# One decode step of cached attention beside an MLP: all pairs in the loops, K awaited by TensorE, K folded in two chunks

## The chip, the cores and the metric

The kernel runs on one core of one Trainium2 chip. A core has a matrix engine (TensorE, in the profile PE, its weight loads PEld), three engines for elementwise work (VectorE = DVE, ScalarE = ACT, GpSimd = POOL), a sync engine (SyncE = SP) that here only issues transfers, and 16 DMA engines that bring data from HBM into the on-chip memory. The engines run their own instruction streams and meet at semaphores. The metric is the device time of one execution in microseconds.

## The reference

One token for each of 8 sequences passes attention over a cache of 4096 keys in 32 heads of 128, and an MLP; both are added to the input. K and V together are 2 x 8 x 32 x 4096 x 128 bf16 numbers, 537 MB.

```python
x = A_x                                  # (8, 1, 640) bf16
xn = _layernorm(x)
q = (xn @ wq) -> (8, 32, 1, 128)
scores = einsum("bhqd,bhkd->bhqk", q, k_cache) * 128 ** -0.5
o = einsum("bhqk,bhkd->bhqd", softmax(scores), v_cache)
y = _layernorm(xn)
out = x + o.reshape(8, 1, 4096) @ wo + gelu(y @ w1 + b1) @ w2 + b2
```

## The kernel before

**Pairs.** The work is cut into 32 pairs i = (group of 8 heads, sequence). A pair has 8 heads x 4096 keys; its K is a tile of 128 partitions x 256 columns x 128 numbers, 8.4 MB, and so is its V. Each partition holds 256 keys of one head (16 partitions a head). K goes alternately to the slots KA and KB, V to the one slot VS.

**One pair.** GpSimd spreads the query (`qrep`), TensorE turns it into one row per partition (`pe_qbc`), ScalarE copies it out of PSUM (`act_qbc`). The scores of the last 80 of the 256 columns come from TensorE: ten tiles of eight columns are transposed (`pe_T`), evacuated by ScalarE (`act_T`) and multiplied by the query (`pe_QK`); VectorE masks and sums these products (`dve_sel`). The scores of the first 176 columns come from VectorE: in chunks, K times the query in place, a first addition of halves, and a reduction (`dve_chunk`, three chunks of 58, 59 and 59 columns). Then VectorE finds the maxima and writes one bias per head (`dve_max`), ScalarE takes eight exponentials with their sums (`act_exp`), TensorE adds the sums over partitions (`pe_RS`) and multiplies the probabilities with V in 256 small products (`pe_PV`), VectorE inverts the sum (`dve_rinv`), ScalarE copies the product (`act_O`) and GpSimd scales it (`o_norm`).

**Order.** Each step is entered in a list with a position, `at(position, step, ...)`, 100 for a pair; sorted by position, the list gives each engine's order. In the stretch of pair i, ScalarE has the exponentials of pair i-1 (position 90 of the pair before) ahead of the tiles of pair i, TensorE the tiles of pair i ahead of the PV product of pair i-1. Pair 0 is the exception: its exponentials stand at `o + Q + 45`, behind the tiles of pair 1.

**Transfers.** SP issues in the order K(i+1), V(i), K(i+2), V(i+1). K(i) waits until TensorE and VectorE have finished with pair i-2 (`kt`, `km`), V(i) until the PV product of pair i-1 has ended. K1 and V0 wait for the last product of Q with wq (`qw`). TensorE does not wait for K itself: GpSimd waits for the transfer, writes one word (`k_ready`, the tile `kr_sb`), and TensorE waits for that write.

**Loops.** The steps are first recorded as calls, then replayed. ScalarE and VectorE replay pairs 0 and 1 as straight code and the pairs from 2 on in a loop of 15 turns of two pairs (`LOOP0, LOOPN = 2, 15`, `_replay_loop`). TensorE replays pair 0's first part as straight code and then loops (`_replay_pe`): in turn r the first part of pair r (query, tiles), then the sums and PV of pair r-1, and in the last but one turn a block of the end's products, skipped in the others. Semaphore values that grow from turn to turn are computed from the turn's number.

**Head and end.** Before pair 0 come the two norms, the spread of w1 into the layout that TensorE wants (`spread_w1`, five instructions on VectorE and five on ScalarE), the MLP, and Q. At the end the outputs of the first 24 heads are regrouped by products (`pe_sel`) that VectorE folds (`dve_fold`), and multiplied with wo; the last eight follow after PV(31). All instructions are emitted by one helper, so the profile puts nearly all of them on line 111; tiles tell them apart.

Of the kernel before, what the change touches and what calls it, by code (L numbers as in the profile page):

```python
# [14 lines left out]
P = 128  # L15
# [12 lines left out]
class _Eng:  # L28
# [17 lines left out]
    def sig(self, inst):  # L46
        self.n += 1
        inst.call[3] = (self.sem, 1)
        return (self.sem, self.n)

    def wait(self, *tickets):
        best = {}
        for t in tickets:
            if t is None:
                continue
            if isinstance(t, list):
                for u in t:
                    if u is not None:
                        best[u[0]] = max(best.get(u[0], 0), u[1])
            else:  # L60
                best[t[0]] = max(best.get(t[0], 0), t[1])
        for sem, n in best.items():
            if n > self.waited.get(sem, 0):
                self.waited[sem] = n
                self.wait_ge(sem, n)

# [96 lines left out]
def _replay_pe(e, calls, head, mid, end, late):  # L163

    n = len(head)
    first = [calls[a:b] for a, b in zip(head, mid)]
    second = [calls[a:b] for a, b in zip(mid, head[1:] + [end])]
    g1, g2 = _steps(first[:-1]), _steps([[c for c in t if not _late(c, late)] for t in second])
    _replay(e, calls[:head[0]])
    with e.bass.Fori(1, n + 1, engines=OrderedEngineSet([e.engine])) as r:  # L170
        reg = e.to_reg(r)
        with e.If_lt(reg, n):
            for call, step in zip(first[0], g1):
                _emit(e, call, call[1][1] + (r - 1) * step if step else None, r)
        g = iter(g2)
        for call in second[0]:
            if _late(call, late):
                e.wait_ge(call[1][0], (r >> (n.bit_length() - 1)) * 16 + 1)
            else:
                step = next(g)  # L180
                _emit(e, call, call[1][1] + (r - 1) * step if step else None)
        with e.If_eq(reg, n - 1):
            _replay(e, first[-1])
# [8 lines left out]
def bass_parallel_sum__gqa_block_cached__mixer_channel_mlp__decode_kernel(  # L192
# [29 lines left out]
    LOOP0, LOOPN = 2, 15  # L222
# [19 lines left out]
    group0 = [0]  # L242
    for i_ in range(NQ):
        group0.append(group0[-1] + jp_of(i_) // TPB)
# [4 lines left out]
    with ExitStack() as es:  # L249
# [23 lines left out]
        w2_sb = scratch(F * D // P + 2 * PAD)  # L273
# [13 lines left out]
        iota_h = scratch(2 * HS).bitcast(I32)  # L287
        mtmp = scratch(2 * 2 * HS).bitcast(F32).rearrange("p (w n) -> p w n", w=2)
        ones_sb = scratch(B, 1)
        zeros_sb = scratch(P)  # L290
# [3 lines left out]
        Sd_sb = sb("Sd_sb", [P, 2, NKEY], F32)  # L294
# [3 lines left out]
        qbc_sb = sb("qbc_sb", [P, 2, DH], BF)  # L298
        oT_sb = sb("oT_sb", [P, H, B], BF)
        oS_sb = sb("oS_sb", [P, NL, HS, B], BF)  # L300
        oU_sb = sb("oU_sb", [P, 2, HS], F32)
# [3 lines left out]
        mx_sb = sb("mx_sb", [P, 32], F32)  # L305
        mxT_sb = sb("mxT_sb", [P, 32], F32)
        mq_sb = sb("mq_sb", [P, 2], F32)
        mb_sb = sb("mb_sb", [P, 32], F32)
        mbT_sb = sb("mbT_sb", [P, 32], F32)
        NB_sb = sb("NB_sb", [P, 2, HS], F32)  # L310
# [3 lines left out]
        kr_sb = sb("kr_sb", [P, 1], F32)  # L314
# [25 lines left out]
        tk = {}  # L340
# [12 lines left out]
        def load_k(i):  # L353
            s = kslot(i)
            if i >= 2:
                sp.wait(tk[("kt", i - 2)], tk[("km", i - 2)])
            elif s == KB:
                sp.wait(tk["qw"])
            tk[("k", i)] = ld_s[s].sig(sp.dma_start(tile[s], cache_src(A_k_cache, i)))

# [13 lines left out]
        def load_wl(q):  # L374
            sp.wait(tk[("kt", NQ - 2)], tk[("km", NQ - 2)])
# [12 lines left out]
        def consts_pool():  # L388
            pool.iota(iota_h, [[-HP, HS]], base=0, channel_multiplier=1)
            tk["iota"] = pool.sig(pool.iota(iota_i, [[1, P]], base=0, channel_multiplier=-1))  # L390
            for d, (ap, v) in zip([None] * (6 - len(ld_vl)) + ld_vl, (
                    (zeros_sb, 0.0), (w2_sb[:, 0:PAD], 0.0), (w2_sb[:, PAD + F * D // P:], 0.0), (ones_sb, 1.0),
                    (mx_sb[:, :], 0.0), (mb_sb[:, :], 0.0))):
# [5 lines left out]
        def sel_pool():  # L399
            pool.wait(tk["id"], tk[("kt", NQ - 2)], tk[("km", NQ - 2)])  # L400
# [23 lines left out]
        def idents():  # L424
            dve.wait(tk["iota"])
            tk["id"] = dve.sig(dve.tensor_scalar(ident_bf[:, :], iota_i, 0.0, None, ALU.is_equal))
            dve.tensor_scalar(mtmp[:, 0, :], iota_h, 0.0, None, ALU.is_ge)
            t = dve.sig(dve.tensor_scalar(mtmp[:, 1, :], iota_h, float(HP), None, ALU.is_lt))
            dve.wait(t)
            t = dve.sig(dve.tensor_tensor(mask_sb[:, :], mtmp[:, 0, :], mtmp[:, 1, :], ALU.mult))  # L430
            dve.wait(t)
            tk["mask"] = dve.sig(dve.tensor_scalar(off_sb[:, :], mask_sb[:, :], 1.0, 1e30, ALU.subtract, ALU.mult))
            dve.wait(tk["id"])
# [40 lines left out]
        def spread(eng, dst, src, w):  # L474
            n = src.shape[1]
            for k in range(n):
                s_ = src[:, k, :].rearrange("p (q r) -> p r q", r=FQ)[:, w * FH:w * FH + FH + 1, :]
                d_ = dst[:, k, :, :].rearrange("p j (q w) -> p w j q", w=2)[:, w, :, :]
                last = eng.activation(d_, s_, ACT.Copy) if eng is act else eng.tensor_copy(d_, s_)
            return eng.sig(last)  # L480

        def spread_w1(w):
            eng = act if w else dve
            eng.wait(tk["w1"])
            tk[("w1r", w)] = spread(eng, w1r_sb, w1_sb, w)

        def spread_b1():
            pool.wait(tk["b1"])
            for w in range(2):
                tk["b1r"] = spread(pool, b1r_sb, b1_sb, w)  # L490

        def pe_mlp1():
            pe.wait(tk[("w1r", 0)], tk[("w1r", 1)], tk["b1r"], tk["consts"], tk[("xT", 1)])
# [13 lines left out]
        def dve_h():  # L507
            dve.wait(tk["h"], tk["par"])
            for w in range(2):
                last = dve.tensor_scalar(hh_sb[:, w, :, :], hT_sb[:, :, :], par_sb[:, w:w + 1], None, ALU.mult)  # L510
            tk["hh"] = dve.sig(last)
# [13 lines left out]
        def qrep(i):  # L525
            hq, b = divmod(i, B)
            pool.wait(tk["q"], tk.get(("qb_pe", i - 1)), tk.get(("qkl", i - 1)))
            tk[("qrep", i)] = pool.sig(pool.tensor_copy(
                qrep_sb[:, :, :],
                qT_sb[:, hq * HS:(hq + 1) * HS, b][:, :, None].to_broadcast([P, HS, HP])))  # L530

        def k_ready(i):
            pool.wait(tk[("k", i)])
            tk[("kr", i)] = pool.sig(pool.memset(kr_sb[:, :], 0.0))

        def pe_qbc(i):
            pe.wait(tk[("qrep", i)], tk["id"])
# [5 lines left out]
        def act_qbc(i):  # L543
            act.wait(tk.get(("ym", i - 2)))
            QBB.use(act)
            tk[("qb", i)] = QBB.used(act, act.sig(act.activation(
                qbc_sb[:, i % 2, :], QB_ps[:, 0:DH], ACT.Copy)))

        def pe_T(i, t):
            n = group0[i] + t  # L550
            k = n % 2
            j0 = NKEY - jp_of(i) + t * TPB
            pe.wait(tk["id"], tk[("kr", i)])
# [6 lines left out]
        def act_T(i, t):  # L560
            n = group0[i] + t
            k = n % 2
            act.wait(tk.get(("qk", n - NS)))
# [8 lines left out]
        def pe_QK(i, t):  # L572
            n = group0[i] + t
# [12 lines left out]
        def dve_chunk(i, c):  # L586
# [6 lines left out]
                kt, kt, qbc_sb[:, s, :][:, None, :].to_broadcast([P, w, DH]), ALU.mult))  # L593
# [3 lines left out]
            dve.wait(t, tk.get(("exp", i - 2)))  # L597
            tk[("km", i)] = dve.sig(dve.tensor_reduce(Sd_sb[:, s, lo:hi], kt[:, :, 0:DH // 2], AX.X, ALU.add))

        def dve_sel(i, f):  # L600
# [4 lines left out]
            dve.wait(tk["mask"], tk.get(("exp", i - 2)))  # L605
# [6 lines left out]
                Sd_sb[:, s, j0:j0 + hw], sp_, AX.X, ALU.add)))  # L612

        def dve_max(i):
            s = i % 2
            dve.wait(tk[("s", i)], tk[("km", i)], tk["consts"])
            t = dve.sig(dve.tensor_reduce(mx_sb[:, 0:1], Sd_sb[:, s, :], AX.X, ALU.max))
# [10 lines left out]
            dve.wait(t, tk.get(("exp", i - 2)))  # L628
            tk[("nb", i)] = dve.sig(dve.tensor_scalar(
                NB_sb[:, s, :], off_sb[:, :], mbT_sb[:, 0:1], None, ALU.add))  # L630

        def act_exp(i):
            s = i % 2
            act.wait(tk[("nb", i)], tk.get(("pv", i - 1)))
            for h in range(HS):
                last = act.activation(P_sb[:, h, :], Sd_sb[:, s, :], ACT.Exp, bias=NB_sb[:, s, h:h + 1],
# [9 lines left out]
        def dve_rinv(i):  # L646
            if i < 0:
                tk[("ri", i)] = CHB.used(dve, dve.sig(dve.tensor_copy(ri_sb[:, i % 2, :], off_sb[:, :])))
                return
# [19 lines left out]
        def act_O(i):  # L669
            if i < 0:  # L670
                act.wait(tk["mask"])
                tk[("oU", i)] = PVB.used(act, act.sig(act.activation(oU_sb[:, i % 2, :], off_sb[:, :], ACT.Exp)))
                return
            PVB.use(act)
            tk[("oU", i)] = PVB.used(act, act.sig(act.activation(oU_sb[:, i % 2, :], PV_ps[:, 0:HS], ACT.Copy)))

        def o_norm(i):
# [6 lines left out]
            if i < NQ - 1:  # L684
                pool.wait(tk[("oU", i)], tk[("ri", i)])
                tk[("on", i)] = pool.sig(pool.tensor_tensor(dst, oU_sb[:, s, :], ri_sb[:, s, :], ALU.mult))
# [20 lines left out]
        def dve_fold(g):  # L707
            ap, bank = sel_ps(g)
            bank.use(dve)
            view = ap.rearrange("p (h x) -> p h x", h=HS)  # L710
            t = dve.sig(dve.tensor_tensor(
                view, view, mask_sb[:, :, None].to_broadcast([P, HS, HS * B]), ALU.mult))
            dve.wait(t)
            tk[("oS", g)] = bank.used(dve, dve.sig(dve.tensor_reduce(
                oS_sb[:, g, :, :].rearrange("p s b -> p (s b)"), view.rearrange("p h x -> p x h"),
                AX.X, ALU.add)))
# [33 lines left out]

        Q = 100.0
# [18 lines left out]
        at(-771.5, spread_w1, 0)  # L770
        at(-771.5, spread_w1, 1)
# [7 lines left out]
        for i in range(NQ):  # L779
# [6 lines left out]
            at(o - 2, k_ready, i)  # L786
# [20 lines left out]
            at(o + Q + 75, o_norm, i)  # L807
        at(57, dve_rinv, -1)
# [9 lines left out]
        for g in range(NL):  # L818
            at(o + g, pe_sel, g)
            at(o + 0.5 + g, dve_fold, g)  # L820
# [3 lines left out]
        for m in range(LOOPN + 1):  # L824
# [56 lines left out]
```

## Time and profile before

| | |
|---|---|
| median of 3 runs | 1283.59 us (1283.59 to 1283.61) |
| profiled execution | 1283.58 us, span 1282.3 us |
| DMA | 552.00 MB, mean 430 GB/s over the span |
| VectorE busy | 1099.9 us (86%) |
| TensorE matmuls, weight loads busy | 667.4 us (52%), 569.3 us (44%) |
| ScalarE busy, GpSimd busy | 483.8 us (38%), 98.6 us (8%) |
| mean granted TensorE clock | 0.592 |

In a row of the timeline stand the start in us from the span's start, the duration, engine, line, operation, the tile written `<-` the tiles read, the shape, and how many instructions were merged; in brackets the idle time of the engine before it and what ended it ("issue": nothing that the profile shows). In the chain a row is start, duration, what. In the waits a row is who waited for whom: us in total, times, longest. A row of a window gives its length, each engine's busy us (with instructions), the granted clock of TensorE, the DMA share and GB/s. A row of a queue gives packets, MB and the share of 16 engines.

### The profile page before, as it was taken

What the parts mean: (1) busy time and instruction counts of PE and PEld (TensorE: products, weight loads), DVE (VectorE), ACT (ScalarE), POOL (GpSimd) and SP (SyncE); (2) the same over time, 40 slices, a digit from 0 to 9 for tenths busy, and PEclk for the clock granted to TensorE, in tenths of its full rate; (3) what the DMA queues carried; (4) which work ended last, traced back from release to release, by engine and by line L of the source; (5) the groups of instructions that cost most, each with busy time, mean ns of one, the idle gap of its engine ahead of it and who ended that gap; (6) DMA issues with size and microseconds to landing.
All of it is one profiled execution on the core that took longest, in us unless ns stands there. A gap on an engine that the chain in (4) does not pass through costs nothing.

```text
span 1282.3 us, 34538 instructions
## 1 busy us (share of the span) xinstructions
PE 667.4 (52%) x13994; PEld 569.3 (44%) x13994; DVE 1099.9 (86%) x677; ACT 483.8 (38%) x908; POOL 98.6 (8%) x112
## 2 busy tenths in 40 slices
PE   4463555564544664544654544654545655545645
PEld 3352444453443553433553534543434544434545
DVE  3599998988888988888988888988889988889885
ACT  3343333344432344423344423344323444323441
POOL 1011110000000000000000000000000000000001
PEclk9955565565656666556666556665556655556655
DMA  9999999999999999999999999999999999999998
GB/s 401 449 421 434 433 431 431 438 433 431 431 440 431 431 431 440 431 429 433 442 429 429 433 442 429 431 431 442 431 430 431 444 427 433 429 444 427 433 419 358
DMA packets 11509, 552.00 MB, mean 430 GB/s; under 512 B 1245, under 2 KB 2278, under 8 KB 2279
## 3 DMA queue, kind: packets, MB, share of 16 engines
q1 hardware_dynamic: 11424, 551.79, 99.6%
q8 instruction: 9, 0.15, 0.0%
q10 hardware_dynamic: 70, 0.03, 0.0%
q14 instruction: 6, 0.04, 0.0%
HBM read 551.80 MB, written 0.01 MB: 430 GB/s over the span
## 4 chain that ended last, share of the span: by engine, by line
DMA 74%; PE 17%; DVE 7%; issue 1%; ACT 0%; SPq 0%; DVEq 0%; ACTq 0%
DMA S_sb<-in_A_v_cache_dram 69%; PE PV_ps L111 16%; DVE S_sb L111 4%; DMA S_sb<-in_A_k_cache_dram 3%; DVE Sd_sb L111 2%; DMA S_sb<-in_A_wo_dram 2%; PE TR_ps L111 1%; ACT P_sb L111 0%; PE S_ps L111 0%; DVE S_ps L111 0%; SPq L111 0%; ACT KT_sb L111 0%; DVE mx_sb L111 0%; PE ACC_ps L111 0%; DVE mxT_sb L111 0%
## 5 line engine op out<-in xcount | busy, mean ns | idle before, releaser
L111 PE MATMUL TR_ps<-ident_bf,S_sb 128*128 128x128 bf16 (+1 forms) x2570 | 340.6, 270 | 363.5 <-POOL kr_sb L111 344.8
L111 DVE TENSOR_TENSOR S_sb<-S_sb,qbc_sb 128x7552 bf16<-128x7552 bf16 (+1 forms) x96 | 388.7, 4049 | 124.7 <-DMA S_sb<-in_A_k_cache_dram 124.3
L111 PEld LDWEIGHTS TR_ps<-ident_bf,S_sb 128*128 (+2 forms) x2570 | 243.4, 102 | 423.7 <-issue 351.6
L111 DVE TENSOR_REDUCE Sd_sb<-S_sb 128x59 f32<-128x3776 bf16 (+1 forms) x96 | 390.2, 4064 | 6.0
L111 ACT ACTIVATE KT_sb<-TR_ps 128x1024 bf16<-128x1024 bf16 x320 | 327.1, 1024 | 116.6 <-PE TR_ps L111 106.8
L111 PE MATMUL PV_ps<-P_sb,S_sb 128*128 128x8 bf16 x8192 | 224.3, 175 | 144.5 <-DMA S_sb<-in_A_v_cache_dram 140.5
L111 PEld LDWEIGHTS PV_ps<-P_sb,S_sb 128*128 128x128 bf16 x8192 | 221.3, 103 | 147.4 <-DMA S_sb<-in_A_v_cache_dram 143.2
L111 ACT ACTIVATE P_sb<-Sd_sb,NB_sb 128x256 bf16<-128x256 f32 x256 | 126.3, 494 | 229.0 <-DVE NB_sb L111 229.0
L111 DVE TENSOR_TENSOR S_sb<-S_sb 128x3776 bf16<-128x3776 bf16 (+1 forms) x96 | 202.9, 2114 | 3.3
L111 ACT ACTIVATE oU_sb<-PV_ps 128x8 f32<-128x8 f32 x31 | 5.5, 178 | 384.3 <-PE PV_ps L111 384.3
L111 PE MATMUL S_ps<-qrep_sb,KT_sb 128*128 128x8 bf16 x2560 | 121.3, 177 | 51.7 <-ACT KT_sb L111 48.5
L111 PEld LDWEIGHTS S_ps<-qrep_sb,KT_sb 128*128 128x128 bf16 x2560 | 90.7, 101 | 82.1 <-ACT KT_sb L111 35.9
L111 POOL TENSOR_TENSOR oT_sb<-oU_sb,ri_sb 128x8 bf16<-128x8 f32 x31 | 69.3, 2235 | 383.5 <-DVE S_sb L111 341.8
L111 POOL COPY qrep_sb<-qT_sb 128x128 bf16<-128x128 bf16 x32 | 19.7, 615 | 477.6 <-PE S_ps L111 451.4
L111 ACT ACTIVATION_READ_ACCUMULATOR P_sb<-Sd_sb,NB_sb 128x1 f32 x256 | 47.8, 187 | 0.0
L111 DVE TENSOR_REDUCE Sd_sb<-S_ps 128x40 f32<-128x320 f32 x64 | 31.4, 491 | 2.2
L111 DVE TENSOR_TENSOR S_ps<-S_ps,mask_sb 128x320 f32<-128x320 f32 (+1 forms) x66 | 32.7, 495 | 0.0
L111 POOL MEMSET kr_sb<- 128x1 f32 x32 | 3.1, 98 | 293.4 <-DMA S_sb<-in_A_k_cache_dram 293.4
L111 ACT ACTIVATE qbc_sb<-QB_ps 128x128 bf16<-128x128 f32 x32 | 8.9, 278 | 41.8 <-PE QB_ps L111 41.8
L111 PE MATMUL QB_ps<-ident_bf,qrep_sb 128*128 128x128 bf16 x32 | 9.1, 284 | 26.1 <-DVE S_sb L111 15.0
L111 PE MATMUL CH_ps<-rs_sb,ones_f 128*128 128x8 f32 x64 | 15.4, 313 | 4.6 <-ACT P_sb L111 4.2
L111 PEld LDWEIGHTS QB_ps<-ident_bf,qrep_sb 128*128 128x128 bf16 x32 | 3.3, 104 | 29.0 <-ACT oU_sb L111 21.0
(58 smaller groups left out, 142.4 us busy)
## 6 DMA issues: line engine op xcount, KB each, us to landing
S_sb<-in_A_wq_dram SPq DMA_DIRECT2D x1, 5120.0 KB, 25.4
S_sb<-in_B_w_dram SPq DMA_DIRECT2D x2, 2160.0 KB, 11.1
S_sb<-in_A_v_cache_dram SPq DMA_DIRECT2D x1, 4096.0 KB, 15.3
S_sb<-in_A_v_cache_dram SPq DMA_DIRECT2D x1, 2816.0 KB, 18.6
S_sb<-in_A_wo_dram SPq DMA_DIRECT2D x1, 2560.0 KB, 31.2
S_sb<-in_A_wo_dram SPq DMA_DIRECT2D x1, 1280.0 KB, 33.9
S_sb<-in_A_v_cache_dram SPq DMA_DIRECT2D x1, 1280.0 KB, 21.4
S_sb<-in_A_wo_dram SPq DMA_DIRECT2D x1, 640.0 KB, 22.6
```

The lines of the kernel that those rows point to most:

```text
L111: inst = getattr(e, name)(*a, **k)
```

## The change

All 32 pairs go through the loops: ScalarE loops over single pairs from 0 on, VectorE over two pairs from 0 on, TensorE over 33 turns, in the first of which the second part is skipped. So that the first turn's waits are defined, a pair -1 is made up: its steps are run through the recorder without emitting anything, and a few real instructions raise their semaphores by the counts that this pair would have raised. One step of it is real, the exponentials of pair -1 on ScalarE, on zeros; two small products of TensorE (`pe_first`) define the PSUM areas that are read for it. The exponentials of pair 0 take the place that those of the other pairs have.

GpSimd's `k_ready` goes; TensorE waits for the two K semaphores itself, once per pair, with values computed from the turn. K's load waits for VectorE alone. The fold of K has two chunks (117 and 59 columns). Query row, scores, biases and the copied PV product have one buffer instead of two, so their writers wait for the readers one pair back. In the head, w1 is spread by ScalarE alone in two instructions, the mask comes from the identity by one reduction, and some small tiles are set by one instruction. At the end, two of the three folds are done together.

```diff
 def _replay_pe(e, calls, head, mid, end, late, parity):
-    with e.bass.Fori(1, n + 1, engines=OrderedEngineSet([e.engine])) as r:
+    with e.bass.Fori(0, n + 1, engines=OrderedEngineSet([e.engine])) as r:
...
         with e.If_lt(reg, n):
...
+                if _late(call, parity):
+                    k = [x is call[1][0] for x in parity].index(True)
+                    e.wait_ge(call[1][0], ((r + 2 - k) >> 1) * 16 + k)
...
-        g = iter(g2)
-        for call in second[0]:
+        with e.If_ne(reg, 0):
+            g = iter(g2)
+            for call in second[1]:
...
         with e.If_eq(reg, n - 1):
             _replay(e, first[-1])
...
-    LOOP0, LOOPN = 2, 15
...
     def chunks(i):
         jd = NKEY - jp_of(i)
-        n = 3
-        return [(jd * c // n, jd * (c + 1) // n) for c in range(n)]
+        return [(0, jd * 2 // 3), (jd * 2 // 3, jd)]
...
         def load_k(i):
             s = kslot(i)
             if i >= 2:
-                sp.wait(tk[("kt", i - 2)], tk[("km", i - 2)])
+                sp.wait(tk[("km", i - 2)])
             elif s == KB:
                 sp.wait(tk["qw"])
...
-        def spread_w1(w):
-            eng = act if w else dve
-            eng.wait(tk["w1"])
-            tk[("w1r", w)] = spread(eng, w1r_sb, w1_sb, w)
+        def spread_w1():
+            act.wait(tk["w1"])
+            for w in range(2):
...
+                last = act.activation(d_, s_, ACT.Copy)
...
-        def k_ready(i):
-            pool.wait(tk[("k", i)])
-            tk[("kr", i)] = pool.sig(pool.memset(kr_sb[:, :], 0.0))
...
         def act_qbc(i):
-            act.wait(tk.get(("ym", i - 2)))
+            act.wait(tk[("ym", i - 1)])
...
         def pe_T(i, t):
-            pe.wait(tk["id"], tk[("kr", i)])
+            if t == 0:
+                pe.wait(*tk[("kk", i)])
...
-            dve.wait(t, tk.get(("exp", i - 2)))
-            tk[("km", i)] = dve.sig(dve.tensor_reduce(Sd_sb[:, s, lo:hi], kt[:, :, 0:DH // 2], AX.X, ALU.add))
+            dve.wait(t, tk[("exp", i - 1)])
+            tk[("km", i)] = dve.sig(dve.tensor_reduce(Sd_sb[:, lo:hi], kt[:, :, 0:DH // 2], AX.X, ALU.add))
...
         def act_O(i):
-            if i < 0:
-                act.wait(tk["mask"])
-                tk[("oU", i)] = PVB.used(act, act.sig(act.activation(oU_sb[:, i % 2, :], off_sb[:, :], ACT.Exp)))
-                return
             PVB.use(act)
+            act.wait(tk[("on", i - 1)], tk[("ri", i)])
...
+        def pe_first():
+            pe.wait(tk["consts"], tk["mask"])
+            tk["pe_spare"] = pe.matmul(PV_ps[:, 0:HS], ident_bf[:, :], ident_bf[:, 0:HS], start=True, stop=True)
+            CHB.use(pe)
+            tk["first"] = CHB.used(pe, pe.sig(pe.matmul(RS_ps, ones_f[:, :], mask_sb[:, :], start=True, stop=True)))
...
             at(o + 2, dve_chunk, i, 0)
-            at(o + 26, dve_chunk, i, 1)
             at(o + 52, dve_sel, i, 0)
             at(o + 55, dve_sel, i, 1)
-            at(o + 58, dve_chunk, i, 2)
+            at(o + 58, dve_chunk, i, 1)
             at(o + 84, dve_max, i)
-            at(o + 90 if i else o + Q + 45, act_exp, i)
+            at(o + 90, act_exp, i)
...
+        at(-744, pe_first)
+        at(-15, made_up)
+        at(-10, act_exp, -1)
...
-            at(o + 0.5 + g, dve_fold, g)
+        at(o + 1.5, dve_fold, 0, 2)
+        at(o + 2.5, dve_fold, 2, 1)
```

More of the change, by code (lines that the diff above doesn't have):

```diff
@@ L604, in dve_sel @@
             j0 = NKEY - jp_of(i) + t0 * TPB
-            dve.wait(tk["mask"], tk.get(("exp", i - 2)))
+            dve.wait(tk[("exp", i - 1)])
             SBK[f].use(dve)
@@ L627, in dve_max @@
             t = dve.sig(dve.transpose(mbT_sb[:, :], mb_sb[:, :]))
-            dve.wait(t, tk.get(("exp", i - 2)))
+            dve.wait(t, tk[("exp", i - 1)])
             tk[("nb", i)] = dve.sig(dve.tensor_scalar(
-                NB_sb[:, s, :], off_sb[:, :], mbT_sb[:, 0:1], None, ALU.add))
+                NB_sb[:, :], off_sb[:, :], mbT_sb[:, 0:1], None, ALU.add))
         def act_exp(i):
             s = i % 2
-            act.wait(tk[("nb", i)], tk.get(("pv", i - 1)))
+            act.wait(tk[("nb", i)], tk[("pv", i - 1)])
             for h in range(HS):
-                last = act.activation(P_sb[:, h, :], Sd_sb[:, s, :], ACT.Exp, bias=NB_sb[:, s, h:h + 1],
+                last = act.activation(P_sb[:, h, :], Sd_sb[:, :], ACT.Exp, bias=NB_sb[:, h:h + 1],
                                       scale=SCALE, accum_out=rs_sb[:, h:h + 1])
@@ L831, in mark @@
             pe.waited = {}
-        for i in range(1, NQ + 1):
+        for i in range(NQ + 1):
             at(i * Q - 12, mark, head)
```

224 lines of the change are left out of this document (142 added, 82 removed).

## The prediction

> **What bounds the kernel now.** I read the page first, for the shares and the chain's summary, then the chain in order of time, the sync engine's issues, the waits, and last the stretch from 0 to 140 us instruction by instruction.
>
> ```profile
> span 1282.3 us, 34538 instructions
> ...
> q1 hardware_dynamic: 11424, 551.79, 99.6%
> q8 instruction: 9, 0.15, 0.0%
> ...
> DMA 74%; PE 17%; DVE 7%; issue 1%; ACT 0%; SPq 0%; DVEq 0%; ACTq 0%
> ```
>
> The queue that carries K, V and the weights keeps 16 engines busy for 99.6% of the span. The chain (74% DMA, 17% TensorE) looks mixed; in order of time it alternates, here for two pairs late in the loop:
>
> ```profile
> 1061.13 31.63 DMA S_sb<-in_A_v_cache_dram
> ...
> 1092.81 7.01 PE PV_ps L111 x256
> ...
> 1099.84 31.62 DMA S_sb<-in_A_v_cache_dram
> ```
>
> V is issued when the PV product of the pair before has emptied its only slot, and lands 31.6 us later. One pair takes 1099.84 - 1061.13 = 38.71 us and moves a K and a V, so 19.35 us each. V's 31.6 us therefore hold 31.6 - 19.35 = 12.3 us of waiting behind the K already in the queue. That is the cover of a late V issue. Averages and waits say the same:
>
> ```profile
> 241.30:1247.60 1006.30, 525.40 (x10894) 446.29 (x10894) 880.40 (x521) 383.20 (x728) 71.94 (x77) 0.58 1.00 433
> ```
>
> ```profile
> PE PV_ps L111 <- DMA S_sb<-in_A_v_cache_dram: 140.5, 30, 5.2
> DVE S_sb L111 <- DMA S_sb<-in_A_k_cache_dram: 124.3, 28, 9.7
> ```
>
> From 241 to 1248 us the DMA share is 1.00 at 433 GB/s. TensorE waits 140.5/30 = 4.7 us a pair for V, VectorE 124.3/28 = 4.4 us for K. So inside the loop nothing is won by less work, and nothing lost by up to some 4 us more on either chain. What can move the time is whether the queue runs empty. The issues of the head show how near it comes:
>
> ```profile
> 2.12 34.34 SPq L111 DMA_DIRECT2D S_sb<-in_A_k_cache_dram  x2
> 36.50 0.43 SPq L111 DMA_DIRECT2D S_sb<-in_A_v_cache_dram  x1
> 79.08 0.33 SPq L111 DMA_DIRECT2D S_sb<-in_A_k_cache_dram  x1
> 96.64 0.33 SPq L111 DMA_DIRECT2D S_sb<-in_A_v_cache_dram  x1
> ...
> 138.44 0.33 SPq L111 DMA_DIRECT2D S_sb<-in_A_v_cache_dram  x1
> ...
> 1067.69 0.33 SPq L111 DMA_DIRECT2D S_sb<-in_A_k_cache_dram  x1
> ```
>
> They are K0 with K1 (K1 at the end of that piece, 36.1 us), V0, K2, V1, V2, and a K of the steady loop. Landings of K show as GpSimd's mark for it:
>
> ```profile
> 46.33 0.10 POOL L111 MEMSET kr_sb<- 128x1 f32 x1 [9.41 <-DMA S_sb<-in_A_k_cache_dram]
> ...
> 65.99 0.10 POOL L111 MEMSET kr_sb<- 128x1 f32 x1 [5.30 <-DMA S_sb<-in_A_k_cache_dram]
> ...
> 144.58 0.10 POOL L111 MEMSET kr_sb<- 128x1 f32 x1 [3.03 <-DMA S_sb<-in_A_k_cache_dram]
> ```
>
> From K1 (65.99) to K3 (144.58) four transfers land, 19.65 us each, so V0 lands near 85.6 and K2 near 105.3.
>
> **The change, part by part.** *The order of pair 0 and 1 on ScalarE.* Before, the exponentials of pair 0 were placed behind the transposed tiles of pair 1; a loop over all pairs puts them ahead, as in every other pair. Then PV(0) must wait for exp(0) and for pair 1's ten tiles:
>
> ```profile
> 54.83 3.95 ACT L111 ACTIVATE KT_sb<-TR_ps 128x1024 bf16<-128x1024 bf16 x4 [0.34 <-PE TR_ps L111]
> 58.80 1.28 ACT L111 ACT_TABLE_LOAD   x1
> 66.70 0.49 DVE L111 TENSOR_TENSOR S_ps<-S_ps,mask_sb 128x320 f32<-128x320 f32 x1
> ...
> 80.67 0.51 ACT L111 ACTIVATE P_sb<-Sd_sb,NB_sb 128x256 bf16<-128x256 f32 x1 [0.49 <-DVE NB_sb L111]
> 84.53 0.19 ACT L111 ACTIVATION_READ_ACCUMULATOR P_sb<-Sd_sb,NB_sb 128x1 f32 x1
> ...
> 114.92 0.51 ACT L111 ACTIVATE P_sb<-Sd_sb,NB_sb 128x256 bf16<-128x256 f32 x1 [10.75 <-DVE NB_sb L111]
> ```
>
> Pair 1 already runs in that order: exp(1) starts at 114.92, V2 is issued at 138.44, 23.5 us later. Exp(0) starts at 80.67, some 0.2 us earlier with three VectorE instructions fewer in the fold; 80.45 + 23.5 = 104.0 us for V1's issue, against 96.64. Its cover was K2's landing at 105.3. How long an issue into an empty queue needs is shown by the first load:
>
> ```profile
> 0.75 0.61 ACTq L111 DMA_DIRECT2D S_sb<-in_A_x_dram  x1
> ...
> 2.76 0.88 DVE L111 BATCH_NORM_STATS2 S_sb<-S_sb 8x6 f32<-8x320 bf16 x2 [0.59 <-DMA S_sb<-in_A_x_dram]
> ```
>
> 2.0 us for ten KB. So V1 is late by 104.0 + 2.0 - 105.3 = 0.7 us. Bounds: 0, if half of the 2.0 us overlaps the end of K2; 1.7 us, if a restart of 16 engines costs 1 us more than one small load. I take 0.7. Queue time lost here comes back nowhere, since all that follows is at 1.00.
>
> *The turn before the first.* ScalarE runs a made-up exp(-1) between pair 0's query copy and its tiles: 84.53 + 0.19 - 80.67 = 4.05 us, and a table load of 1.28 us ahead of it. Tiles of pair 0 ended at 54.83 + 3.95 = 58.78; from a query copy at 46.0 (below) they end near 46.0 + 5.3 + 11.2 = 62.5, and the last products near 63. VectorE wants them at 66.70: cover 3.7 us, cost 0. TensorE's two extra dummy products lie under VectorE's copy of Q.
>
> *The spread of w1* moves from two engines to one, ten instructions become two.
>
> ```profile
> 9.57 8.39 ACT L111 ACTIVATE S_sb<-S_sb 128x896 bf16<-128x896 bf16 x5 [2.59 <-DMA S_sb<-in_B_w_dram]
> 9.57 5.21 DVE L111 COPY S_sb<-S_sb 128x896 bf16<-128x896 bf16 x5
> ...
> 36.14 0.42 DVE L111 CAST qT_sb<-CH_ps 128x256 bf16<-128x256 f32 x1 [12.53 <-PE CH_ps L111]
> ...
> 37.29 0.28 ACT L111 ACTIVATE qbc_sb<-QB_ps 128x128 bf16<-128x128 f32 x1 [14.13 <-PE QB_ps L111]
> 46.30 4.02 DVE L111 TENSOR_TENSOR S_sb<-S_sb,qbc_sb 128x7424 bf16<-128x7424 bf16 x1 [9.74 <-DMA S_sb<-in_A_k_cache_dram]
> ```
>
> ScalarE's own row doubled is 16.8 us; VectorE's price for the other half would give 13.6. I take 16.8: Q comes 8.4 us later, at 44.5, and with it the issues of K1 and V0; the query copy ends at 37.57 + 8.4 = 46.0, 0.3 us before VectorE can start on K0 (46.30). K1's bytes count from 44.5 + 2.0 = 46.5, where K0 landed at 46.3: 0 to 0.2 us. That cover is used up: each further us of spread costs a us.
>
> *Code that TensorE has not run yet.* TensorE stands still at places where no data is late:
>
> ```profile
> 27.44 0.58 PEld L111 LDWEIGHTS ACC_ps<-S_sb 128*128 128x128 bf16 x19 [0.58 <-issue]
> ...
> 27.95 2.98 PEld L111 LDWEIGHTS CH_ps<-S_sb 128*128 128x128 bf16 x109
> ...
> 34.57 1.44 PEld L111 LDWEIGHTS CH_ps<-S_sb 128*128 128x128 bf16 x51 [3.64 <-issue]
> ...
> 85.42 5.71 PEld L111 LDWEIGHTS PV_ps<-P_sb,S_sb 128*128 128x128 bf16 x211
> 95.23 1.28 PEld L111 LDWEIGHTS PV_ps<-P_sb,S_sb 128*128 128x128 bf16 x45 [4.11 <-issue]
> ...
> 103.57 0.10 PEld L111 LDWEIGHTS QB_ps<-ident_bf,qrep_sb 128*128 128x128 bf16 x1 [7.06 <-issue]
> ```
>
> Between the first two stops lie 19 + 109 = 128 weight loads and as many matmuls, 256 instructions; the q8 queue fetched 9 pieces of 0.15/9 MB, 17 KB each. I read the stops as code in pieces of 256 instructions, fetched one ahead: 34.57 - 27.44 = 7.1 us a piece. The 4.11 us inside PV(0) and the 7.06 us behind it (the jump over the last block) are that; no later turn has them. Before, neither cost anything, as V1 had 105.3 - 2.0 - 96.64 = 6.7 us in hand. After, the prologue loses pair 0's copy. By my count of instructions the loop's first part runs from about 880 to 1310, the PV part to 1840, the last block to 2130; a piece begins at 1280, 1536, 1792, 2048. Turn 0 enters the piece at 1280 shortly before it jumps, so the next piece, with most of PV, is fetched 30 us ahead: I take no stop in PV(0). The two jumps of turn 0 land in cold pieces, 2 x 7.1 us from 63: 77.2, query product and copy to 78, where VectorE and exp(0) need it at 80.4. Cover 2.4 us, cost 0. Bounds: 0, and 4.1 us (PV(0) stops as before).
>
> [...]
>
> *One piece of code fewer* (8 for 9): K0 to K1 took 65.99 - 46.33 = 19.66 where 19.35 would do; I take 0.2 us gained, between 0 and 0.4.
>
> *K awaited by TensorE* drops GpSimd's mark. Behind the wait stand only K's own transposes; GpSimd's query copy and the normalisation come free. It gains tenths of a us under the 4.7 us wait for V: 0. *K's load* waits for the fold alone: a K issued at 1067.69 has some 25 us in hand (V's 12.3 with another 19.35, less the 6.6 us between the issues): 0. *Two chunks for three*: one pair's three instructions less are under VectorE's 4.4 us wait: 0. *Single copies* of the query, the scores, the biases and PV's output: each now waits for the reader one pair back, which by program order ended before (exp ends near K's landing, the fold writes scores 12 us later): 0; if a wait bit, it had 4 us.
>
> *The tail.* Two folds signal together, so the output product of the first comes about 1.2 us later. Behind it stands PV(31), which waits for V anyway:
>
> ```profile
> 1273.31 2.52 PE L111 MATMUL PV_ps<-P_sb,S_sb 128*128 128x8 bf16 x88 [0.82 <-DMA S_sb<-in_A_v_cache_dram]
> 1276.44 1.24 PE L111 MATMUL PV_ps<-P_sb,S_sb 128*128 128x8 bf16 x40 [0.62 <-DMA S_sb<-in_A_v_cache_dram]
> ```
>
> 0.82 and 0.62 us absorb it: 0.
>
> Sum: 0.7 + 0.1 - 0.2 = +0.6 us on 1283.58 for the profiled execution (span 1282.3, 1.3 us around it), which is the median of the runs to 0.01: 1284.2. About 0.2%, 2.6 us, is what I count as no change.
>
> **Rivals.** *PV(0) stops for its code after all* (slower): the jump drops the fetch, or my count is 30 instructions off. Place: after the first 100 products of PV(0). Price 4.1 us: V1 at 108.1, +4.7, 1288.3. It decides from 2.0 us of stop on. The same sum holds if the cold jumps take 21 us instead of 14 (exp(0) then starts 4 us late). For it: the row at 95.23; against it: turn 0 walks by that code early.
>
> *A table load every turn.* The trace has three in all, and the third (58.80) stands in straight code before the loop; the warm-up that it served is gone, so gelu's table stands at the loop's door and exp's at its end. 1.28 us on ScalarE each turn; hidden under the 4.7 us in the loop, but ahead of exp(0) it makes V1 +2.0: 1285.5. If it stands ahead of the query copy it is free. [...]
>
> *A single copy or the table load outgrows the cover*, and the loop becomes bound by TensorE: 31 turns times the excess: 1 us too much makes 1314.6. Against it: 4.7 us a pair.
>
> *Faster*: the queue has nothing to give but the 4 x 0.3 us of K1 to K3 and the code, at most 1.5 us: 1282.1; more would need a change in the rate.
>
> **How the numbers follow.** Forecast 0.46; PV(0) stop or slow jumps 0.37; table load in front of exp(0) alone 0.09; a loop bound by an engine 0.05; a gain over 0.2% 0.03. The forecast and the table load (1285.5) stay within 0.2%: same 0.55, slower 0.37 + 0.05 = 0.42, faster 0.03. The range begins at 1283.0 (restart 0, the code piece 0.4, and 0.2 for what the counts leave open) and ends at 1289.0 (the stop of 4.1 us with 0.7 us of a dearer restart); left out are the loop case, the gain, and the stop together with a table load or slow jumps, under 2 in 10.
>
> **What would show it.** Right: V1 issued near 104 with PV(0) unbroken; two stops of 7 us between 63 and 78; K1 issued near 44.5; 38.7 us a pair; 8 code fetches. Wrong: an "issue" stop in PV(0); table loads over 3; VectorE starting after 46.5; V waits under 3 us a pair.

## The result, and the profile after

The changed kernel takes 1289.33 us (median; 1288.76 to 1292.19), the kernel before 1283.61 beside it: a ratio of 1.0048 with a 95% interval of 1.0033 to 1.0063. It is slower by 5.7 us. The forecast was 1284.2. The time is 0.3 us above the upper end of the range, on the side of a rival and not of the forecast. The profiled execution took 1289.32 us with a span of 1287.8, against 1283.58 and 1282.3 before.

The steady loop is as it was. First the page of the kernel after, then its waits, its chain in order of time and its long window, to be held against the rows of the prediction:

```profile
span 1287.8 us, 34642 instructions
...
q1 hardware_dynamic: 11424, 551.79, 99.3%
q8 instruction: 11, 0.18, 0.1%
...
DMA 76%; PE 17%; DVE 4%; issue 2%; ACT 0%; SPq 0%; DVEq 0%; ACTq 0%
```

```profile
PE PV_ps L128 <- DMA S_sb<-in_A_v_cache_dram: 141.3, 31, 5.2
DVE S_sb L128 <- DMA S_sb<-in_A_k_cache_dram: 135.9, 30, 4.7
```

```profile
169.40 7.01 PE PV_ps L128 x256
176.43 31.64 DMA S_sb<-in_A_v_cache_dram
208.11 7.01 PE PV_ps L128 x256
```

```profile
246.70:1253.00 1006.30, 532.70 (x10894) 453.37 (x10894) 870.61 (x443) 416.45 (x754) 48.47 (x51) 0.53 1.00 433
```

A pair still takes 208.11 - 169.40 = 38.71 us, the queue still moves 433 GB/s from 247 to 1253 us, and both waits on DMA are there (141.3/31 = 4.6 us for V, 135.9/30 = 4.5 for K). The new lines are the eleven pieces of code where there were nine, and a queue share of 99.3% where it was 99.6. So the 5.7 us were lost in the head. The sync engine's issues and TensorE's timeline there (start, duration, instruction; in brackets the idle time ahead of it and what ended it) show where:

```profile
2.19 41.44 SPq L128 DMA_DIRECT2D S_sb<-in_A_k_cache_dram  x2
43.67 0.43 SPq L128 DMA_DIRECT2D S_sb<-in_A_v_cache_dram  x1
78.84 0.33 SPq L128 DMA_DIRECT2D S_sb<-in_A_k_cache_dram  x1
107.54 0.33 SPq L128 DMA_DIRECT2D S_sb<-in_A_v_cache_dram  x1
112.78 0.33 SPq L128 DMA_DIRECT2D S_sb<-in_A_k_cache_dram  x1
```

```profile
77.66 0.10 PEld L128 LDWEIGHTS QB_ps<-ident_bf,qrep_sb 128*128 128x128 bf16 x1 [15.78 <-issue]
...
97.01 3.16 PE L128 MATMUL PV_ps<-P_sb,S_sb 128*128 128x8 bf16 x113
103.07 3.56 PE L128 MATMUL PV_ps<-P_sb,S_sb 128*128 128x8 bf16 x127 [2.90 <-issue]
106.93 0.57 PE L128 MATMUL PV_ps<-P_sb,S_sb 128*128 128x8 bf16 x16 [0.30 <-issue]
...
111.19 0.28 PE L128 MATMUL QB_ps<-ident_bf,qrep_sb 128*128 128x128 bf16 x1 [3.68 <-issue]
```

V1 is issued at 107.54, where it was 96.64. PV(0), whose end releases it, starts at 97.01 and stands still twice, 2.90 and 0.30 us, with no data late. What that does to the queue is one row of windows, first of the kernel after, then of the kernel before (the last two columns are the DMA share and GB/s):

```profile
102.50:108.25 5.75, 4.13 (x143) 3.96 (x143) 5.72 (x3) 0.26 (x2) 0.29 (x1) 0.50 0.03 6
```

```profile
102.50:108.25 5.75, 1.17 (x8) 0.80 (x8) 5.72 (x4) 0.28 (x1) 3.90 (x2) 0.50 0.90 388
```

For 5.75 us hardly a packet begins, where the kernel before moves 388 GB/s. A packet is counted where it begins (a window of 0.25 us further down shows a DMA share of 10.29 for it), so the queue empties a little later than this row says: by the trace the 16 parts of K2 land between 103.26 and 105.34 us, V1's first packets begin at 108.50, and between 96 and 120 us the queue moves 336 GB/s, against 436 in the kernel before: (436 - 336) x 24 / 436 = 5.5 us of the queue's time. Nothing gives the loss back: the product that runs at 208.11 here runs at 202.62 in the chain of the kernel before, 5.5 us earlier, and the two spans differ by 5.5 us as well.

ScalarE's rows settle two smaller points:

```profile
9.46 15.72 ACT L128 ACTIVATE S_sb<-S_sb 128x4480 bf16<-128x4480 bf16 x2 [2.94 <-DMA S_sb<-in_B_w_dram]
...
43.91 1.28 ACT L128 ACT_TABLE_LOAD   x1 [12.21 <-DVE qT_sb L128]
45.20 0.28 ACT L128 ACTIVATE qbc_sb<-QB_ps 128x128 bf16<-128x128 f32 x1
```

The spread of w1 takes 15.72 us on ScalarE alone, and a table load stands ahead of the query copy, as in each later turn (34 loads in all, below).

### The profile page after: what moved, and what is told of

Its sections match the earlier page's. It is cut to its first block, busy times and chain, and to the rows that moved or that the text cites. A ratio compares the mean times of both kernels' runs of the same rounds, so it can differ in the third digit from the quotient of the medians.

```text
span 1287.8 us, 34642 instructions
## 1 busy us (share of the span) xinstructions
PE 677.2 (53%) x13997; PEld 577.3 (45%) x13997; DVE 1083.1 (84%) x573; ACT 534.8 (42%) x952; POOL 65.3 (5%) x77
## 3 DMA queue, kind: packets, MB, share of 16 engines
q1 hardware_dynamic: 11424, 551.79, 99.3%
## 4 chain that ended last, share of the span: by engine, by line
DMA 76%; PE 17%; DVE 4%; issue 2%; ACT 0%; SPq 0%; DVEq 0%; ACTq 0%
DMA S_sb<-in_A_v_cache_dram 71%; PE PV_ps L128 16%; DMA S_sb<-in_A_k_cache_dram 3%; DVE S_sb L128 3%; DMA S_sb<-in_A_wo_dram 2%; DVE ini_sb L128 1%; PE TR_ps L128 1%; ACT P_sb L128 0%; PE S_ps L128 0%; SPq L128 0%; DVE S_ps L128 0%; ACT KT_sb L128 0%; PE ACC_ps L128 0%; DVE mbT_sb L128 0%; DVE mxT_sb L128 0%
## 5 line engine op out<-in xcount | busy, mean ns | idle before, releaser
L128 DVE TENSOR_TENSOR S_sb<-S_sb,qbc_sb 128x14976 bf16<-128x14976 bf16 x64 | 384.0, 5999 | 136.3 <-DMA S_sb<-in_A_k_cache_dram 135.9
L128 PEld LDWEIGHTS TR_ps<-ident_bf,S_sb 128*128 (+1 forms) x2570 | 246.2, 102 | 417.7 <-issue 355.3
L128 DVE TENSOR_REDUCE ini_sb<-S_sb 128x117 f32<-128x7488 bf16 x64 | 385.3, 6020 | 5.1
L128 PE MATMUL PV_ps<-P_sb,S_sb 128*128 128x8 bf16 x8192 | 224.5, 175 | 144.5 <-DMA S_sb<-in_A_v_cache_dram 141.3
L128 ACT ACTIVATE P_sb<-ini_sb 128x256 bf16<-128x256 f32 x264 | 130.2, 494 | 173.3 <-DVE ini_sb L128 173.3
L128 POOL TENSOR_TENSOR oT_sb<-oU_sb,ri_sb 128x8 bf16<-128x8 f32 x31 | 49.3, 1591 | 403.7 <-ACT oU_sb L128 403.7
L128 ACT ACT_TABLE_LOAD x34 | 43.6, 1283 | 33.7 <-DVE qT_sb L128 12.2
L128 POOL COPY qrep_sb<-qT_sb 128x128 bf16<-128x128 bf16 x32 | 9.3, 292 | 789.4 <-PE S_ps L128 755.8
L128 ACT ACTIVATION_READ_ACCUMULATOR P_sb<-ini_sb 128x1 f32 x264 | 49.3, 187 | 0.0
L128 DVE TENSOR_REDUCE ini_sb<-S_ps 128x40 f32<-128x320 f32 x64 | 31.4, 491 | 2.2
L128 PE MATMUL CH_ps<-S_sb 128*128 128x8 bf16 x244 | 9.4, 170 | 18.5 <-ACT S_sb L128 15.6
L128 ACT ACTIVATE S_sb<-S_sb 8x1 f32<-8x1 f32 (+1 forms) x4 | 16.1, 4058 | 5.8 <-DMA S_sb<-in_B_w_dram 2.9
```

What stands on the lines that cost most here:

```text
L128: inst = getattr(e, name)(*a, **k)
```

## The experiments

The theory after the result: the 5.7 us are V1's late issue, and V1 is late for two reasons: PV(0) starts at 97, and PV(0) stands still for code that has not arrived. Its rivals: the table loads, the other parts of the change, and, for the stops, that the code's mere size and not its place brings them. Each difference to the kernel before is to its own runs on the same chip.

**The order of exp(0) alone**, put into the kernel before:

```diff
-            at(o + 90 if i else o + Q + 45, act_exp, i)
+            at(o + 90, act_exp, i)
```

> The kernel before with one position changed: exp(0) ahead of pair 1's tiles, as in every other pair. Theory A (V1 meets an empty queue; both the order and code that TensorE has not run yet make it late): PV(0) starts near 97 and stops in its code here too, although the loops are the old ones; V1 is issued between 107.5 and 110 instead of 96.64, and the time rises by 5 to 8 us to 1289-1291.5. Rival C (only the new loop, by the jumps of its first turn, makes TensorE's code late): PV(0) runs unbroken, V1 at 104.0, +1 to +2 us, 1284.6-1285.6. Rival B (the loss sits in the loop: table loads, single copies): no change, 1283.6.

Measured: 1289.27 us, ratio 1.0044 (1.0027 to 1.0061), +5.7 us. TensorE and the sync engine:

```profile
98.38 2.36 PE L111 MATMUL PV_ps<-P_sb,S_sb 128*128 128x8 bf16 x83
102.67 4.86 PE L111 MATMUL PV_ps<-P_sb,S_sb 128*128 128x8 bf16 x173 [1.93 <-issue]
...
107.56 0.33 SPq L111 DMA_DIRECT2D S_sb<-in_A_v_cache_dram  x1
```

The order by itself gives the whole loss, in the old loops: PV(0) begins at 98.38 instead of near 85, a stop follows (the kernel before has one too, 128 products further on), and V1 goes out at 107.56.

**The order undone in the changed kernel**: ScalarE runs pairs 0 and 1 in straight code again, exp(0) behind pair 1's tiles, and all else stays changed.

```diff
-            at(o + 90, act_exp, i)
+            at(o + 90 if i else o + Q + 45, act_exp, i)
...
-                if n == "act" or i % 2 == 0:
+                if i >= 2 if n == "act" else i % 2 == 0:
```

> The changed kernel with the order on ScalarE undone: pairs 0 and 1 as straight code, exp(0) behind pair 1's tiles, the loop from pair 2; TensorE and VectorE as changed. Theory A with two causes, each enough by itself: TensorE comes back from the jumps of turn 0 only at about 77.7, so pair 1's tiles end near 91.5, exp(0) near 95, PV(0) starts near 95.3 and stops for its last piece of code; V1 at 104 to 107, 1286.3 to 1288.7, so most of the loss stays. If the order alone were the cause: V1 near 96.6, 1283.6 to 1284.

Measured: 1289.52 us, 1.0046 (1.0029 to 1.0062), +5.9.

```profile
78.07 0.28 PE L128 MATMUL QB_ps<-ident_bf,qrep_sb 128*128 128x128 bf16 x1 [14.38 <-issue]
...
97.05 3.16 PE L128 MATMUL PV_ps<-P_sb,S_sb 128*128 128x8 bf16 x113
103.49 4.17 PE L128 MATMUL PV_ps<-P_sb,S_sb 128*128 128x8 bf16 x143 [3.27 <-issue]
```

That is above the 1286.3 to 1288.7 that I expected, with V1 at 107.68, not at 104 to 107. So the order is enough for the loss, but not needed for it. TensorE's own loop from pair 0 on is a second, independent cause: its two jumps cost 14.4 us and the tiles of pair 1 come that much later. PV(0) stands behind them in TensorE's program and starts near 97 in both orders, here at 97.05 because exp(0) follows the tiles, in the changed kernel at 97.01.

**Both undone**: the edit above, and TensorE's first pair back in straight code with its loop from turn 1. The other parts (K awaited by TensorE, K's load, two chunks, single copies, the spread of w1, the tail) stay.

```diff
-    _replay(e, calls[:head[0]])
-    with e.bass.Fori(0, n + 1, engines=OrderedEngineSet([e.engine])) as r:
+    _replay(e, calls[:mid[0]])
+    with e.bass.Fori(1, n + 1, engines=OrderedEngineSet([e.engine])) as r:
...
-        with e.If_ne(reg, 0):
```

> The run before this one with TensorE's first pair taken out of the loop again as well (straight code, loop from turn 1); all other parts of the change stay: K awaited by TensorE, two chunks, single copies, w1 spread by ScalarE alone, the folds of the end. Theory A: V1 near 96.6, no gap in the queue, 1283.2 to 1284.2, the time of the kernel before. If any of the other parts costs something: that much more, up to 1289.3.

Measured: 1284.09 us, 1.0003 (0.9994 to 1.0013), +0.5.

```profile
90.01 5.64 PE L128 MATMUL PV_ps<-P_sb,S_sb 128*128 128x8 bf16 x206
98.51 1.51 PE L128 MATMUL PV_ps<-P_sb,S_sb 128*128 128x8 bf16 x50 [2.85 <-issue]
...
100.04 0.33 SPq L128 DMA_DIRECT2D S_sb<-in_A_v_cache_dram  x1
```

The remaining parts cost nothing that this measurement can tell. PV(0) still stops 2.85 us and V1 goes out at 100.04, later than the 96.6 expected, but in time: the queue does not run dry (its row is shown further down). A stop costs only what reaches beyond the cover.

**One table load less a turn**: the changed kernel with a small exponential ahead of ScalarE's loop.

```diff
+        def warm_exp():
+            act.wait(tk["mask"])
+            act.activation(oU_sb[:, :], off_sb[:, :], ACT.Exp)
...
+        at(-743, warm_exp)
```

> The changed kernel with one small exponential ahead of ScalarE's loop, so that exp's table is loaded before the loop and none is needed in it: 3 or 4 table loads instead of 34. Theory A: each load stands ahead of the query copy in idle time, so nothing moves: 1288.7 to 1290. Rival B: 31 loads of 1.28 us less on ScalarE bring back 1 to 5 us.

Measured: 1289.73 us, 1.0049 (1.0032 to 1.0066). The groups of this kernel, then those of the kernel after:

```profile
L128 ACT ACT_TABLE_LOAD x3 | 3.8, 1283 | 6.9 <-PE CH_ps L128 5.0 <-issue 1.9
```

```profile
L128 ACT ACT_TABLE_LOAD x34 | 43.6, 1283 | 33.7 <-DVE qT_sb L128 12.2
```

31 loads go, and no time with them. That rival falls.

**Does the place of the code decide the stop?** Idle matrix products ahead of the MLP on TensorE move all later code along. In the kernel after, 128 weight loads and 127 products lie between the two stops of PV(0), which I read as a piece of 256 instructions (128 products). By that reading a piece ends at product 113 of PV; the piece before it began 226 - 256 = 30 instructions ahead of PV, of which, by my count of the program, 21 come before the end of the loop's first part, where turn 0 jumps away. 20 idle products are 40 instructions: turn 0 then jumps 61 instructions after it has entered that piece.

```diff
+            for _ in range(20):
+                pe.matmul(PV_ps[:, 0:HS], zeros_sb, zeros_sb[:, 0:HS], start=True, stop=True)
```

> The changed kernel with 20 idle products (40 instructions) ahead of the MLP on TensorE, in a time when it waits for w1; nothing else. If the stops in PV(0) are pieces of 256 instructions arriving late: the first stop moves from behind product 113 to behind product 93 and the second from 240 to 220, with V1 between 107 and 109. If they belong to these products or to their data: they stay at 113 and 240.

Measured: 1285.66 us, 1.0016 (1.0005 to 1.0026), +2.0.

```profile
97.55 6.98 PE L128 MATMUL PV_ps<-P_sb,S_sb 128*128 128x8 bf16 x256
...
104.56 0.33 SPq L128 DMA_DIRECT2D S_sb<-in_A_v_cache_dram  x1
```

I had expected the stops to move; they vanished. PV(0) runs unbroken from nearly the same start, and eight pieces of code are fetched:

```profile
q8 instruction: 8, 0.13, 0.0%
```

This is the state that the prediction had forecast, with V1 at 104.56 for 104.0. It separates the two reasons: the late start of PV(0) costs at most 2.0 us, the stops the other 3.7 or a little more. (At most, because K1 too is issued later here, near 44.5 for 43.6: over the first 96 us the queue moves 419 GB/s, for 422 in the changed kernel.) Two more kernels, with 8 and with 128 idle products in the same place, tested whether place or amount does it:

> 8 idle products are 16 instructions: turn 0 jumps 37 instructions after it has entered a piece, where 21 lost the next piece and 61 kept it. By my theory one of the two known cases comes: PV(0) unbroken, V1 near 104.6, +2.0 us on the kernel before (1285.6), if 37 are enough; or stops at products 105 and 233, V1 near 107.5, +5.7 (1289.3), if not. By the rival, in which the loss shrinks with the amount of added code, PV(0) would stop for about half as long and the time lie between, near 1287.5.

> 128 idle products are 256 instructions, one whole piece of code: TensorE's loop then starts at the same place within a piece as in the changed kernel, and turn 0 again jumps some 21 instructions after it has entered a piece. If that place decides (my theory), the stops in PV(0) come back at products 113 and 241, V1 is issued near 107.5 and the time is that of the changed kernel, 1288.8 to 1290. If it was the additional code or the delay that saved the prefetch with 20 idle products (the rival), PV(0) runs unbroken, V1 is issued near 104.6 and the time is 1285.2 to 1286.1.

Measured: 1289.48 us (1.0046, 1.0029 to 1.0063) with 8, and 1289.91 us (1.0051, 1.0034 to 1.0068) with 128. TensorE with 8, then with 128:

```profile
97.25 2.94 PE L128 MATMUL PV_ps<-P_sb,S_sb 128*128 128x8 bf16 x105
101.27 3.56 PE L128 MATMUL PV_ps<-P_sb,S_sb 128*128 128x8 bf16 x127 [1.08 <-issue]
106.87 0.79 PE L128 MATMUL PV_ps<-P_sb,S_sb 128*128 128x8 bf16 x24 [2.04 <-issue]
```

```profile
97.23 3.16 PE L128 MATMUL PV_ps<-P_sb,S_sb 128*128 128x8 bf16 x113
103.57 4.16 PE L128 MATMUL PV_ps<-P_sb,S_sb 128*128 128x8 bf16 x143 [3.18 <-issue]
```

With 128, a whole piece, the code has its old place again, and the stop at product 113, the late V1 (107.76) and the loss are back, with more code and more idle work than in the gaining kernel. With 8 the boundary moves by 8 products, as counted, and the stops stay (V1 at 107.68). So it is the place of the code and not its amount, and the effect is not gradual: by my count the step lies between 37 and 61 instructions from the entry of a piece to the jump. Idle products move everything behind them, the places where the jumps land too, and more instructions also take more time; so that the distance from the entry to the first jump is what acts is a reading, not shown apart from these.

**V1 held back, in the kernel before**: V1 also waits for VectorE's fold of K1. The first kernel was meant to hold it until the end of the fold, but at its place in the order the wait meets the second of three chunks, so V1 goes out at 101.22 and the case that its expectation speaks of did not come about. The second kernel moves the issue behind the last chunk, and V1 goes out at 113.41.

```diff
+            if i == 1:
+                sp.wait(tk[("km", 1)])
...
-            at(o + 50, load_v, i)
+            at(o + 70 if i == 1 else o + 50, load_v, i)
```

(The first kernel has the wait alone, the second both edits.)

> The kernel before, with V1 held back until VectorE has finished the fold of pair 1 (113.3 us), so that the queue runs empty for a known time; nothing else is changed. If a restart costs 2.0 us, as the prediction had it from the first small load: late by 113.3 + 2.0 - 105.3 = 10.0 us, 1293.6. If it is dearer, as the changed kernel suggests (V1 at 107.54 cost 5.45 us at V2's landing, so loss = issue - 102.1): 11.2 us, 1294.8.

> The kernel before with V1 held back until the last chunk of pair 1's fold (the earlier run of this kind got the second chunk, 101.2 us, and lost 0.9 us): issue at 113.4. By the prediction's restart (2.0 us after the issue, against K2 at 105.3): 10.1 us late, 1293.7. By the loss of 5.45 us at 107.54: 11.3 us, 1294.9. If a fetch of code or something else besides the issue made part of those 5.45 us: below 1293.

Measured: 1284.46 us (1.0006, 0.9996 to 1.0015), +0.9 with an interval that includes 1, and 1294.35 us (1.0084, 1.0067 to 1.0101), +10.7, which lies between the two values expected, 1293.7 and 1294.9. In the second, no packets follow K2's until V1 is issued:

```profile
102.50:114.00 11.50, 2.63 (x17) 1.77 (x17) 11.36 (x7) 0.28 (x1) 3.90 (x2) 0.50 0.01 1
```

A V1 that is late by enough, with nothing else touched, makes a loss of this kind and size.

**V in two transfers**, in the changed kernel: the first 64 of V's 256 columns are loaded as soon as the first 64 products of PV are done.

```diff
-            sp.wait(tk["qw"] if i == 0 else tk[("pv" if i < NQ - 1 else "pvh", i - 1)])
+            sp.wait(tk["qw"] if i == 0 else tk[("pvq" if i < NQ - 1 else "pvh", i - 1)])
...
+                for lo, hi in ((0, VQ), (VQ, NKEY)):
+                    if lo and i:
+                        sp.wait(tk[("pv", i - 1)])
```

> The changed kernel with each V brought by two transfers: the first quarter (64 columns) waits only for the first 64 of the 256 PV products of the pair before, the rest as before for all of them. Theory A: the first quarter of V1 is issued near 98.8, before TensorE stops in PV(0), while K2 is still moving; the rest follows at 107.5, with 4.8 us of transfers in hand from 105; no gap in the queue over 0.5 us, 1283.4 to 1284.5. Rival B: the same time as the changed kernel, 1289.3, since nothing in the loop's work is less.

Measured: 1290.35 us, 1.005 (1.0033 to 1.0067); the expectation failed.

```profile
99.40 12.87 SPq L128 DMA_DIRECT2D S_sb<-in_A_v_cache_dram  x2
...
97.51 3.16 PE L128 MATMUL PV_ps<-P_sb,S_sb 128*128 128x8 bf16 x113
105.29 3.55 PE L128 MATMUL PV_ps<-P_sb,S_sb 128*128 128x8 bf16 x127 [4.61 <-issue]
111.34 0.57 PE L128 MATMUL PV_ps<-P_sb,S_sb 128*128 128x8 bf16 x16 [2.50 <-issue]
```

The first part went out at 99.40 as meant, but PV(0) then stopped for 4.61 and 2.50 us, and the second part came at the end of the same row, 112.3, when the first had run out: the gap moved, it did not go. Splitting costs something of its own (a pair takes 38.79 us here, and 31 times 0.08 is 2.5 us). As a test of the gap it decides nothing.

## Why the prediction was wrong

- **The step that failed: "I take no stop in PV(0)."** The term was 0; the stops were 2.90 and 0.30 us, and V1 went out at 107.54 for 104.0. Mechanism, place and consequence are those of the rival to which I gave 0.37, and one of its two conditions was "my count is 30 instructions off". The count itself was near: it put the piece at 1280 with the jump near 1310, 30 instructions on, where it is 21. What was wrong is the reading that entering a piece shortly before a jump is enough for the next one to be fetched and kept. In the runs 21 and 37 instructions, by my count, went with stops (2.90 and 0.30 us, 1.08 and 2.04 us), and 61 with none. The transfers of the instruction queue (q8) show the rest; first the kernel after from 60 to 95 us and from 95 to 120, then the kernel with 20 idle products from 60 to 95, after which it has none:

```profile
q8 instruction: 3, 0.05, 0.5%
q8 instruction: 4, 0.07, 1.0%
q8 instruction: 4, 0.07, 0.7%
```

  Both kernels fetch for the two jumps and one piece ahead, in the kernel after at 66.76, 74.45 and 81.38. The kernel with idle products has one more in the same stretch, four for three: by count, the piece with most of PV, which then ran unbroken. In the kernel after that transfer is missing and comes at 100.85, as PV(0) runs out of code. Three more follow, at 104.35, 107.93 and 114.23, and the first two bring back code that turn 0 had already run: TensorE waits again at product 241 of PV, in the piece where the first jump had landed, and again at the loop's end, where the second had. So, by count and place, the 11 fetches are the 8 forecast and a second fetch of the three pieces behind the missing one. Whether the jump dropped a fetch or came before it was asked for, and why those pieces had to come again, stays open.
- **The second step: the restart term**, 104.0 + 2.0 - 105.3. By the issue times that were seen, that rule gives 1.3 us at 104.56, 4.2 at 107.54 and 10.1 at 113.41; measured were 2.0, 5.7 and 10.7. So it is 0.6 to 1.5 us short each time, and that is why the rival's 1288.3 and the upper end of 1289.0 were short as well. At 100.04 and 101.22 it gives nothing. Measured were +0.5 and +0.9, whose intervals include a ratio of 1, and in the traces the queue does not run dry there (the kernel after, both causes undone, V1 at 101.22):

```profile
96.00:120.00 24.00, 10.96 (x294) 9.77 (x294) 23.26 (x16) 7.68 (x22) 1.05 (x2) 0.52 0.81 336
96.00:120.00 24.00, 4.56 (x78) 3.62 (x78) 23.27 (x16) 5.99 (x20) 3.67 (x1) 0.50 0.99 425
96.00:120.00 24.00, 3.31 (x43) 2.36 (x40) 23.52 (x18) 5.41 (x20) 3.90 (x2) 0.50 0.99 416
```

  Two things were left out. The 16 engines do not run dry together at 105.3: in the kernel after K2's last packets begin before 102.5, and its parts land from 103.26 to 105.34. And the engines start again in step, which the first round of V1 shows, here in the kernel with 20 idle products, in windows of 0.25 us:

```profile
105.50:105.75 0.25, 0.00 (x0) 0.00 (x0) 0.25 (x1) 0.00 (x0) 0.25 (x1) 0.50 10.29 3408
105.75:106.00 0.25, 0.00 (x0) 0.00 (x0) 0.25 (x1) 0.00 (x0) 0.25 (x1) 0.50 2.39 786
```

  All of the round begins within 0.5 us, 0.9 to 1.4 us after the issue, and takes (10.29 + 2.39) x 0.25 = 3.17 us an engine for (3408 + 786) x 0.25 = 1049 KB; at 433 GB/s that is 2.42 us. The 0.75 us more is in no row that the prediction used. How the remainder divides was not tested; the head's own differences, such as K1's issue, are part of it.
- **Right: the order of exp(0).** It delays PV(0) as forecast: V1 would be at 104.0, and is at 104.56 where no stop comes in between. The prediction missed that TensorE's cold jumps would have made PV(0) as late without it, so that undoing the order alone gains nothing.
- **Right: the two jumps, the spread, the turn before the first.** TensorE is back at 77.66 (77.2 forecast) after 15.78 us (14.2). The spread is 15.72 us (16.8), K1 is issued by 43.6 (44.5). The made-up exponentials hold back the copies of pair 0's tiles, which begin at 49.31 for 47.55 before; the products end at 62.0 (63 forecast) and VectorE wants them at 66.52, so the cover held. The kernel with both causes undone, which keeps the spread, is at +0.5, with an interval that includes 1.
- **Right: the terms at 0 in the loop and the tail.** A pair takes 38.71 us as before, waits for V and K keep 4.6 and 4.5 us, and the difference of 5.5 us at 208 us is that of the whole span. K awaited by TensorE, K's load, the chunks and the single copies show no cost or gain in the kernel with both causes undone (0.9994 to 1.0013). The code piece gained (-0.2) was not seen: eleven pieces for nine.
- **The rival of a table load in each turn** is half right: the loads are there, 34, but ahead of the query copy, where the prediction called them free, and they are. The kernel after has one a turn, the kernel with one exponential ahead of the same loop 3 in all, and the times are 1289.33 and 1289.73 us: by these two, what stood in the table at the loop's entry decided whether the loop loads.

## What to carry to other kernels

Where a queue is the bound at 99.6%, look for the one issue whose cover the change uses up, and price its lateness above the plain gap; here each further us of lateness cost about one once the queue ran dry (+2.0 us with the issue at 104.56, +5.7 at 107.54, +10.7 at 113.41), and 0.6 to 1.5 us came on top. The first pass through a loop that jumps over code cost its fetches here (15.78 us in which TensorE ran nothing), and whether the next stretch of code was there hung on a few dozen instructions (stops with 37 from entry to jump, none with 61). So two kernels that differ only in padding must be compared before such a stop is put down to an edit. An undone edit that gains nothing is no proof of innocence: here either of two edits gave the loss alone, and only undoing both showed it.

## What the runs showed of the hardware that I had not expected

- With a jump 21 or 37 instructions, by my count, after TensorE had entered a piece of code, PV(0) stopped a turn later and 11 pieces were fetched (the kernel after, 8 idle products); with 61 instructions PV(0) ran unbroken and 8 were fetched (20 idle products). Moving the code by 40 instructions with idle products was worth 3.7 us (1285.66 for 1289.33), by 16 or by 256 nothing (1289.48, 1289.91).
- A piece of code came faster while the DMA queue ran dry: from the start of one stretch of PV(0) to the next are 106.93 - 103.07 = 3.9 us in the kernel after, where K2 lands by 105.34 and V1 is not issued yet, and 111.34 - 105.29 = 6.1 us where V's first part was still being moved; the prediction had 7.1 from the head.
- The number of code fetches was not the 8 of the forecast but between 8 (20 idle products) and 12 (128 idle products), 11 in the kernel after; in the kernels before and after none of them comes after 120 us.
- When V1 met an empty queue, the 16 engines ran their first round in step, 3.17 us for what takes 2.42 in the steady loop (20 idle products).
